# A recurrent attention and two MLPs on one core: wider token blocks in the second MLP, another transfer rate in the planner's table, earlier decay loads and a reordered range check

## The chip, the cores and the metric

The kernel runs on one NeuronCore of a Trainium2 chip. The metric is the device time of one execution in microseconds (us). The kernel uses TensorE (PE, with its weight loads shown apart as PEld), VectorE (DVE), ScalarE (ACT) and the DMA engines, whose transfers are nearly all issued from the queue of SyncE (SP). GpSimd (POOL) only fills a few constants at the start.

## The reference, cut to what matters

```python
for t in range(S):                         # per batch and head, D = 48, complex state D x D
    state = a_n[t] * state + outer(k[t], v[t])   # a_n: a scaled to a magnitude of at most 0.999
    y[t] = q[t] @ state.real
x = y as (3072 tokens, 384)
h = x @ w_in;  g = softplus(h);  x2 = g @ w_out          # first MLP, hidden width 2048
out = ((x2 @ w1) * (x2 @ w2)) @ w3 @ w_out2              # second MLP, hidden width 1024
```

There are 4 batches of 768 positions, so 3072 tokens, and 8 heads. The weights arrive as 64-bit floats.

## The kernel before, in words

**Attention.** The sequence is cut into 24 chunks of 128 positions. For chunk u, `load(u)` brings the decay inputs (a tile of 384 KB named `a`), `norm(u)` scales them, `scan` forms running complex products over pairs of chunks in a tile tagged `P`, `inv(u)` forms scaled q and k, and `mm(u)` does the matmuls (`ktp`, `sc`, `yp`, `stp`). The tile tagged `a` has one buffer; only chunk 1 borrows another (`n2`).

**First MLP.** Token blocks of 128, 256 and then seven of 384 tokens (`BLOCKS`, `NB = 384`). For each block 16 hidden slices f: `s1` multiplies into a PSUM tile `s`, ACT and DVE make the softplus, `s2a` accumulates into three PSUM tiles `acc`, and `evac` copies them out and stores them to the DRAM tiles `x2d`. The first two blocks multiply in plain float32, the others split each operand into a high and a low part in the format fp32r and use three products. Weights `wr` (32 loads of 384 KB) are turned from 64 bits to 32 by three DVE instructions.

**Second MLP.** w3 and w_out2 are first multiplied together (`w3_piece`, PSUM tile `wpa`, in three groups of columns with eight pieces k each); the split halves of w_out2 for k = 0 to 3 lie in the two buffers tagged `P`. Then come 8 blocks of 384 tokens. `b_x` loads a block of x2 and splits it (`bxh`, `bxl`, buffers `xh` and `xl` of the pool `sp`). For each of 8 slices, `s3` makes `pb` and `pa` with nine matmuls each, ACT copies `pb` to `be`, DVE multiplies (`bg`), ACT and DVE split (`bgh`, `bgl`), and `s2b` adds nine matmuls into `acc`. Five PSUM buffers of one tag serve `pa` and `pb`.

**Range check.** While the second MLP runs, all weights are loaded again (`ckr`, 80 pieces, three buffers) and DVE finds their smallest and largest squares (`ck`, `lims`). After the last matmul a few small instructions (`okp`, `ok1`, `okt`, `oki`) make one number, which every engine loads to decide whether a slow general path has to run.

**Order.** Nothing of this is issued in the order in which it is written. `Plan` records every instruction, gives it a cost and a landing time (`cost`), runs 16 rounds of list scheduling, and issues the instructions of all engines in the order of the best round. The engines then wait for semaphores only. In the table a transfer of n bytes costs at least n / 360 ns on the queue of SP, and a load of an input lands 2500 + n / 360 ns after its issue. The scheduler also knows which buffer must be free before a tile can be written.

Of the kernel before, what the change touches and what calls it, by code (L numbers as in the profile page):

```python
# [11 lines left out]
F32 = mybir.dt.float32  # L12
F32R = mybir.dt.float32r
I32 = mybir.dt.int32
AF = mybir.ActivationFunctionType
ALU = mybir.AluOpType
PSUM = bass.MemoryType.PSUM
DRAM = bass.MemoryType.DRAM

P = 128  # L20
B, H, SEQ, D = 4, 8, 768, 48
DM = H * D
NT = B * SEQ
T = 128
NCH = NT // T
CPB = SEQ // T
G = DM // P
GT = G * T
FA = 2048 // P
FB = 1024 // P  # L30
KC = DM // P
NB = 384
# [4 lines left out]
GB = 3  # L37
HB = 5
AMB = 2
ATT = 5  # L40
S1B = 5
ATAG = "s1"
YB = 1
VB = 1
# [4 lines left out]
PB = 2  # L49
XB = 2  # L50
# [4 lines left out]
LEAD = 0  # L55
ROUNDS = 16
SEED = 214
NBB = NT // NB

ROW = [128 * (_h // 2) + 64 * (_h % 2) + _d if _h < 6 else 128 * (_d // 16) + 48 + 64 * (_h - 6) + _d % 16  # L60
       for _h in range(H) for _d in range(D)]
# [10 lines left out]
class Plan:  # L72
# [49 lines left out]
    def cost(self, eng, op, outs, ins):  # L122
        n = max(self.free_size(x) for x in (*outs, *ins))
        if eng == "SP":
            size = 4
            for _, n in outs[0].ap:
                size *= n
            cost = max(650 if n < 512 and self.on_chip(ins[0]) else 475, size / 360)
            if not self.on_chip(outs[0]):
                land = 5200  # L130
            elif self.on_chip(ins[0]):
                land = 2300
            elif hasattr(ins[0].tensor, "tag_meta"):
                land = 6800
            else:
                land = 2500 + size / 360
            return cost, max(land - cost, 0)
        if eng == "PE":
            n = self.free_size(outs[0])
            if op == "transpose":  # L140
                return 109, 250
            m = outs[0].ap[0][1]
            if ins[0].dtype == F32R:
                return n / 2.4 + 14, 250
            return (0.75 * n + 24 if m <= 64 else max(n, m) / 0.6 + 5), 250
        if eng == "DVE":
            far = [x for x in ins if x.ap[-1][0] >= 4 and x.ap[-1][1] > 1]
            return 72 + n / (1.92 if op == "tensor_scalar" else 0.52 if len(far) > 1 else 0.95), 200
        if eng == "ACT":
            return 105 + 0.88 * n, 200  # L150
        return 160 + n * 2.08, 200
# [198 lines left out]
def fused(ctx: ExitStack, tc: tile.TileContext, a_in, qk_in, v_in, wio, w12, w3t, wo2, q, k, v, a_re, a_im, outT):  # L350
    nc = tc.nc
    plan = Plan(tc)
    V, A, PE, GP, SP = plan.V, plan.A, plan.PE, plan.GP, plan.SP

    fast = ExitStack()
    dram = ctx.enter_context(tc.tile_pool(name="dram", bufs=1, space=DRAM))
    x2d = [dram.tile([P, KC, NB], F32, name=f"x2d{i}", tag=f"x2d{i}") for i in range(NBB)]

    pd = [dram.tile([2 * DM, 2 * T], F32, name=f"pd{u}", tag=f"pd{u}") for u in range(NCH)]
    xg = dram.tile([DM, NT], F32, name="xg", tag="xg")  # L360
    cp = ctx.enter_context(tc.tile_pool(name="cp", bufs=1))
    wp = fast.enter_context(tc.tile_pool(name="wp", bufs=1))
    sp = fast.enter_context(tc.tile_pool(name="sp", bufs=2))
    ps = fast.enter_context(tc.tile_pool(name="ps", bufs=1, space=PSUM))
    ap = fast.enter_context(tc.tile_pool(name="ap", bufs=1))
# [3 lines left out]
    ident = cp.tile([P, P], F32, name="ident")  # L369
# [10 lines left out]
    m2max = cp.tile([P, NCH], F32, name="m2max")  # L380
    pend = cp.tile([P, B, G], F32, name="pend")
    NCK = 2 * FA + 6 * FB
    wlim = cp.tile([P, 2], F32, name="wlim")
    ncheck = [0]

# [11 lines left out]
    c = [dict() for _ in range(NCH)]  # L397
# [7 lines left out]
    def pst(tag, bufs, shape, name):  # L405
        return ps.tile(shape, F32, tag=tag, bufs=bufs, name=name)
# [3 lines left out]

    def load(u):
        s = c[u]
        s["a"] = ap.tile([P, 2, GT], F32, tag="n2" if u == 1 else "a", bufs=1, name=f"a{u}")
        SP.dma_start(s["a"], a_in[u])

    def load_qk(u):
# [268 lines left out]
    u = 0  # L685
# [6 lines left out]
    for us in groups:  # L692
        n = len(us)
# [113 lines left out]
    def s2(n, f, prods, last):  # L807
        if f == 0:
            for i in range(KC):
                acc[i] = pst(f"acc{i}", 1, [P, NB], "acc")  # L810
        for q, (w, xx) in enumerate(prods):
            for i in range(KC):
                PE.matmul(
                    acc[i][:, 0:n], w[:, i * P : (i + 1) * P], xx,
                    start=(f == 0 and q == 0), stop=(f == last and q == len(prods) - 1),
                )
# [11 lines left out]
    def s2b(f, gg):  # L828
        gh, gl = gg
        wh, wl = (x[:, (f % 2) * DM : (f % 2 + 1) * DM] for x in bwp[f // 2])  # L830
        s2(NB, f, [(wh, gh), (wl, gh), (wh, gl)], FB - 1)

    def evac(n, dst, nm):
        for i in range(KC):
            o = sp.tile([P, NB], F32, tag="e", name=f"xo{nm}_{i}")
            A.copy(o[:, 0:n], acc[i][:, 0:n])
            SP.dma_start(dst(i), o[:, 0:n])

# [82 lines left out]
    for bi in range(nblk):  # L921
        last = bi == nblk - 1
        t0, n = BLOCKS[bi]
        if not last:
            start = att_pos[0]
            goal = att_end[sum(BLOCKS[bi + 1]) // T - 1] + LEAD
        gq = {}
        for f in range(FA):
            if bi == 0:
                if f + 4 < FA:  # L930
                    w_load(f + 4)
                if f + 2 < FA:
                    w_piece(f + 2)
            gq[f] = s1(bi, f)
            if f >= 2:
                s2a(bi, f - 2, gq.pop(f - 2))
            if not last:
                att_to(start + (goal - start) * (f + 1) // FA)
            elif f >= 2:
                while pos < len(st) * (f + 1) // FA:  # L940
                    st[pos]()
                    pos += 1
                if f >= 7 and f - 7 < FB - 2:
                    w12_conv(f - 7)
        for f in (FA - 2, FA - 1):
            s2a(bi, f, gq.pop(f))
        evac(n, lambda i: x2d[t0 // NB][:, i, t0 % NB : t0 % NB + n], f"a{bi}")
    w12_conv(FB - 2)
    w12_conv(FB - 1)

    xb = {}

    def b_x(bi):
        r = ap.tile([P, 2 * H * T], F32, tag="rs1", name=f"xr{bi}")[:, 0 : KC * NB]
        r = r.rearrange("p (k n) -> p k n", k=KC)
        SP.dma_start(r, x2d[bi])
        h, l = (sp.tile([P, KC, NB], F32R, tag=t, bufs=XB, name=f"b{t}{bi}") for t in ("xh", "xl"))
        split(h, l, r)
        xb[bi] = (h, l)

    def s3(bi, f):
        xh, xl = xb[bi]
        pa = pst("s1", S1B, [P, NB], f"pa{bi}_{f}")
        pb = pst(ATAG, ATT, [P, NB], f"pb{bi}_{f}")
        wh, wl = bw[f]
        for o, c0 in ((pb, DM), (pa, 0)):
            i = 0
            for w, xx in ((wh, xh), (wl, xh), (wh, xl)):
                for k in range(KC):
                    PE.matmul(  # L970
                        o, w[:, c0 + k * P : c0 + (k + 1) * P], xx[:, k],
                        start=(i == 0), stop=(i == 3 * KC - 1),
                    )
                    i += 1
        e = sp.tile([P, NB], F32, tag="e", name=f"be_{bi}_{f}")
        A.copy(e, pb)
        g = sp.tile([P, NB], F32, tag="g", bufs=GB, name=f"bg_{bi}_{f}")
        V.tensor_tensor(out=g, in0=pa, in1=e, op=ALU.mult)
        gh = sp.tile([P, NB], F32R, tag="gh", bufs=HB, name=f"bgh_{bi}_{f}")
        gl = sp.tile([P, NB], F32R, tag="gl", bufs=HB, name=f"bgl_{bi}_{f}")  # L980
        split(gh, gl, g)
        return gh, gl

# [13 lines left out]
    for bi in range(NBB):  # L997
        gq = {}
        for f in range(FB):
            gq[f] = s3(bi, f)  # L1000
            if f >= 1:
                s2b(f - 1, gq.pop(f - 1))
            if f == 2 and bi + 1 < NBB:
                b_x(bi + 1)
            it += 1
            while ncheck[0] < min(NCK, NCK * it // nit):
                src, n = cks[ncheck[0]]
                r = raw3(src, n, f"ckr{ncheck[0]}")
                check(r, ap.tile([P, DM], F32, tag="v", bufs=VB, name=f"ck{ncheck[0]}"))
        s2b(FB - 1, gq.pop(FB - 1))  # L1010
        evac(NB, lambda i: outT[i * P : (i + 1) * P, bi * NB : (bi + 1) * NB], f"b{bi}")

    for i, n in enumerate(("min", "max")):
        V.tensor_reduce(
            out=wlim[:, i : i + 1], in_=bst[n], axis=mybir.AxisListType.X, op=getattr(ALU, n)
        )
    plan.flush()
    V, PE = nc.vector, nc.tensor
    fast.close()
    ep = ctx.enter_context(tc.tile_pool(name="ep", bufs=1))  # L1020
    okp = ep.tile([P, B * G + NCH + 2], F32, name="okp")
    c0 = 0
    for src, lim, op in (
        (pend.rearrange("p b g -> p (b g)"), 1e-3, ALU.is_ge),
# [4 lines left out]
        n = src.shape[1]  # L1029
        V.tensor_scalar(out=okp[:, c0 : c0 + n], in0=src, scalar1=lim, scalar2=None, op0=op)  # L1030
        c0 += n
    ok1 = ep.tile([P, 1], F32, name="ok1")
    V.tensor_reduce(out=ok1, in_=okp, axis=mybir.AxisListType.X, op=ALU.min)
    oki = ep.tile([1, 1], I32, name="oki")
    with tc.tile_pool(name="fps", bufs=1, space=PSUM) as fps:
        okt = fps.tile([1, P], F32, name="okt")
        PE.transpose(okt, ok1, ident)
        V.tensor_reduce(out=oki, in_=okt, axis=mybir.AxisListType.X, op=ALU.min)
    ok = nc.values_load(oki[0:1, 0:1], min_val=0, max_val=1)
    with tc.If(ok < 1):  # L1040
        general(tc, q, k, v, a_re, a_im, wio, w12, w3t, wo2, xg, outT)
# [211 lines left out]
```

## Time and profile before

| | us |
|---|---|
| median of 3 executions | 982.17 (980.64 to 984.84) |
| profiled execution, its own time | 979.78 |
| its span, first to last instruction | 978.0 |
| PE busy in the span | 883.5 (90%) |
| DVE busy in the span | 787.4 (81%) |
| granted TensorE clock, mean | 0.994 |

The profiled execution's own time is 1.8 us longer than its span. Busy time of PE is the time covered by matmuls whose ends are modelled and which overlap, so the distance from one start to the next tells what a matmul really takes.

### The profile page before, as it was taken

The numbers are of one execution on the slowest core, as the hardware profiler recorded it, in microseconds if no ns is written. First come the engines' busy times: TensorE is split into PE (matmuls) and PEld (weight loads), VectorE is DVE, ScalarE is ACT, GpSimd is POOL, SyncE is SP. The second block draws the span as 40 slices with busy tenths as digits, with TensorE's granted clock in tenths as the row PEclk, the third lists the DMA queues.
The fourth block names the chain that finished last, engine by engine and source line by source line (L and its number), as shares of the span: only waits on it lengthen the run. The fifth ranks groups of instructions, "written<-read, shape, count | busy, mean of one in ns | idle before, by whom it ended". The sixth has DMA issues, their size and how long they took to land.

```text
span 978.0 us, 16869 instructions
## 1 busy us (share of the span) xinstructions
PE 883.5 (90%) x6169; PEld 859.3 (88%) x6169; DVE 787.4 (81%) x1773; ACT 529.5 (54%) x1132; POOL 5.4 (1%) x13
## 2 busy tenths in 40 slices
PE   0027999899999999999999999999999999999996
PEld 0027888799999999999999999999999999999996
DVE  7999999999999999999888787899788975312212
ACT  4246776677877795876766666833222223323221
POOL 2000000000000000000000000000000000000000
PEclk9998999999999999999999999999999999999999
DMA  9763736444573644537262855375788783000000
GB/s 343 244 170 66 189 96 139 125 107 112 164 161 95 161 108 133 156 72 200 82 166 73 191 165 153 106 200 186 250 251 265 238 252 123 24 26 25 1 25 28
DMA packets 84619, 138.68 MB, mean 142 GB/s; under 512 B 8112, under 2 KB 56880, under 8 KB 84528
## 3 DMA queue, kind: packets, MB, share of 16 engines
q1 hardware_dynamic: 84528, 137.53, 50.1%
q8 instruction: 50, 0.82, 0.4%
q14 instruction: 41, 0.34, 0.1%
HBM read 108.00 MB, written 28.31 MB: 139 GB/s over the span
## 4 chain that ended last, share of the span: by engine, by line
PE 64%; DVE 10%; DMA 7%; issue 2%; ACT 1%; SPq 0%; DVEq 0%; ACTq 0%
PE acc L194 23%; PE s L194 14%; PE pa L194 8%; PE pb L194 8%; PE sc L194 3%; PE yp L194 3%; PE wpa L194 3%; DMA a<-a_in 2%; DVE tm L194 2%; DMA ckr<-wio 2%; DVE P L194 2%; DMA ckr<-w 1%; PE stp L194 1%; DVE ck L194 1%; DVE g L194 1%
## 5 line engine op out<-in xcount | busy, mean ns | idle before, releaser
L194 DVE TENSOR_TENSOR tm<-P 128x90 f32<-128x90 f32 (+3 forms) x240 | 145.8, 616 | 1.1
L194 ACT ACTIVATE e<-e 128x384 f32<-128x384 f32 (+2 forms) x288 | 136.2, 486 | 2.9
L194 DVE TENSOR_TENSOR bg<-pa,be 128x384 f32<-128x384 f32 x64 | 35.3, 555 | 91.2 <-PE pa L194 68.4
L194 ACT ACTIVATE e<-s 128x384 f32<-128x384 f32 (+2 forms) x144 | 64.3, 450 | 44.4 <-PE s L194 37.2
L194 DVE TENSOR_TENSOR P<-tm 128x45 f32<-128x45 f32 (+11 forms) x304 | 85.8, 343 | 1.3
L194 ACT CAST bgh<-bg 128x384 fp32r<-128x384 f32 x64 | 32.7, 514 | 93.1 <-DVE bg L194 93.0
L194 DVE SCALAR_TENSOR_TENSOR g<-s,e 128x384 f32<-128x384 f32 (+2 forms) x144 | 73.3, 513 | 12.0 <-ACT e L194 11.8
L194 PE MATMUL ktp<-ident,qkp 128*128 128x128 f32 x120 | 20.9, 289 | 66.0 <-DVE qkp L194 64.4
L194 PEld LDWEIGHTS ktp<-ident,qkp 128*128 128x128 f32 x120 | 15.6, 148 | 68.6 <-issue 57.5
L194 ACT CAST gh<-g 128x384 fp32r<-128x384 f32 x112 | 56.5, 509 | 25.1 <-DVE g L194 18.3
L194 ACT COPY be<-pb 128x384 f32<-128x384 f32 x64 | 30.5, 480 | 71.6 <-PE pb L194 68.7
L194 DVE TENSOR_TENSOR gl<-g,gh 128x384 fp32r<-128x384 f32 x112 | 61.8, 559 | 4.4 <-ACT gh L194 2.7
L194 DVE CUSTOM_DVE_ANT_0 ck<-ckr 128x384 f32<-128x384 f32 x80 | 43.4, 543 | 19.2 <-DMA ckr<-wio 6.5
L194 PE MATMUL sc<-rs 112*128 112x128 f32 x384 | 53.0, 285 | 4.3 <-ACT y L194 1.7
L194 PEld LDWEIGHTS sc<-rs 112*128 112x128 f32 x384 | 50.3, 198 | 6.2 <-ACT y L194 1.9
L194 DVE TENSOR_TENSOR bgl<-bg,bgh 128x384 fp32r<-128x384 f32 x64 | 35.2, 555 | 15.8 <-ACT bgh L194 15.6
L194 DVE TENSOR_REDUCE lims<-ck 128x1 f32<-128x384 f32 x80 | 43.0, 537 | 2.0
L194 PE MATMUL yp<-am,v 128*48 128x128 f32 x384 | 36.9, 282 | 4.4 <-issue 3.2
L194 ACT COPY xob<-acc 128x384 f32<-128x384 f32 x24 | 11.4, 481 | 52.5 <-PE acc L194 37.4
L194 PE MATMUL wpa<-wo,w 128*128 128x384 f32 x192 | 39.1, 334 | 0.0
L194 PE MATMUL s<-x,w 128*128 128x128 f32 (+1 forms) x192 | 36.0, 330 | 3.1 <-ACT x L194 2.2
L194 ACT ACTIVATE nt<-a 128x768 f32<-128x768 f32 x24 | 20.3, 845 | 31.9 <-DMA a<-a_in 31.8
(323 smaller groups left out, 2581.3 us busy)
## 6 DMA issues: line engine op xcount, KB each, us to landing
pd<-qkp SPq DMA_DIRECT2D x24, 768.0 KB, 4.4
rs<-pd SPq DMA_DIRECT2D x48, 384.0 KB, 6.1
wr<-wio SPq DMA_DIRECT2D x32, 384.0 KB, 5.5
ckr<-wio SPq DMA_DIRECT2D x32, 384.0 KB, 3.6
a<-a_in SPq DMA_DIRECT2D x24, 384.0 KB, 3.7
qk<-qk_in SPq DMA_DIRECT2D x24, 384.0 KB, 3.9
w3r<-w3t SPq DMA_DIRECT2D x16, 384.0 KB, 3.5
w12r<-w SPq DMA_DIRECT2D x16, 384.0 KB, 3.3
```

The source lines that it names most:

```text
L194: getattr(engine.unit, op)(*args, **kw)
```

## The change

- The second MLP works in 6 blocks of 512 tokens. Each block is read from one or two of the `x2d` tiles. Its split halves lie in the two `P` buffers (even blocks) or in `wb6` and `wb7` (odd blocks). `be` and `bg` share one tile out of `wa12` to `wa15`, which also hold the evacuated outputs, and `bgh` and `bgl` share one buffer of `xh` or `xl`, four in turn.
- The planner's table counts transfers at 270 bytes per ns in place of 360, in the queue's cost and in the landing time of inputs.
- The decay inputs of chunks 2 and 3 have buffers of their own (`xl`), so their loads need not wait for an earlier chunk.
- The last instructions of the range check are recorded in the plan, and use buffers that are already there, instead of being issued after it in new ones.

```diff
+NX = 512
+NBB = NT // NX
...
-            cost = max(650 if n < 512 and self.on_chip(ins[0]) else 475, size / 360)
+            cost = max(650 if n < 512 and self.on_chip(ins[0]) else 475, size / 270)
...
-                land = 2500 + size / 360
+                land = 2500 + size / 270
...
     def load(u):
         s = c[u]
-        s["a"] = ap.tile([P, 2, GT], F32, tag="n2" if u == 1 else "a", bufs=1, name=f"a{u}")
+        if u in (2, 3):
+            t = sp.tile([P, KC, NB], F32, tag="xl", bufs=XB, name=f"a{u}")
+            s["a"] = t.rearrange("p k n -> p (k n)")[:, 0 : 2 * GT].rearrange("p (c n) -> p c n", c=2)
+        else:
+            s["a"] = ap.tile([P, 2, GT], F32, tag="n2" if u == 1 else "a", bufs=1, name=f"a{u}")
...
     def b_x(bi):
...
-        SP.dma_start(r, x2d[bi])
-        h, l = (sp.tile([P, KC, NB], F32R, tag=t, bufs=XB, name=f"b{t}{bi}") for t in ("xh", "xl"))
+        n0 = 0
+        while n0 < NX:
+            i, o = divmod(bi * NX + n0, NB)
+            n = min(NB - o, NX - n0)
+            SP.dma_start(r[:, :, n0 : n0 + n], x2d[i][:, :, o : o + n])
+            n0 += n
+        if bi % 2:
+            h, l = (wp.tile([P, KC, NX], F32R, tag=f"wb{i}", name=f"bx{i}_{bi}") for i in (6, 7))
+        else:
+            h, l = (ap.tile([P, KC, NX], F32R, tag="P", bufs=PB, name=f"bx{i}_{bi}") for i in "hl")
...
+    def b_room(name):
+        return wp.tile([P, 2 * DM], F32, tag=f"wa{12 + next(nbf) % 4}", name=name)[:, 0:NX]
+
+    def b_pair(name):
+        t = sp.tile([P, KC, NB], F32R, tag=("xh", "xl")[next(nbg) % 2], bufs=XB, name=name)
+        t = t.rearrange("p k n -> p (k n)")
+        return t[:, 0:NX], t[:, NX : 2 * NX]
...
-        e = sp.tile([P, NB], F32, tag="e", name=f"be_{bi}_{f}")
-        A.copy(e, pb)
-        g = sp.tile([P, NB], F32, tag="g", bufs=GB, name=f"bg_{bi}_{f}")
-        V.tensor_tensor(out=g, in0=pa, in1=e, op=ALU.mult)
-        gh = sp.tile([P, NB], F32R, tag="gh", bufs=HB, name=f"bgh_{bi}_{f}")
-        gl = sp.tile([P, NB], F32R, tag="gl", bufs=HB, name=f"bgl_{bi}_{f}")
+        g = b_room(f"bg_{bi}_{f}")
+        A.copy(g, pb)
+        V.tensor_tensor(out=g, in0=pa, in1=g, op=ALU.mult)
+        gh, gl = b_pair(f"bgg_{bi}_{f}")
         split(gh, gl, g)
...
-    plan.flush()
-    V, PE = nc.vector, nc.tensor
-    fast.close()
-    ep = ctx.enter_context(tc.tile_pool(name="ep", bufs=1))
-    okp = ep.tile([P, B * G + NCH + 2], F32, name="okp")
+    okp = ap.tile([P, DM], F32, tag="v", bufs=VB, name="okp")
...
+    okt = pst("s1", S1B, [P, NB], "okt")[0:1, 0:P]
+    PE.transpose(okt, ok1, ident)
+    V.tensor_reduce(out=oki, in_=okt, axis=mybir.AxisListType.X, op=ALU.min)
+    plan.flush()
+    fast.close()
```

## Rows read from the trace of the kernel before

**Rows 1.** Part 1 of the page: busy time, share, instructions.

```profile
PE 883.5 (90%) x6169; PEld 859.3 (88%) x6169; DVE 787.4 (81%) x1773; ACT 529.5 (54%) x1132; POOL 5.4 (1%) x13
```

**Rows 2.** Windows by stage: from:to length, busy of each engine, PEclk, DMA share, GB/s.

```profile
0.00:57.50 57.50, 0.00 (x0) 0.01 (x1) 51.06 (x106) 18.39 (x32) 5.42 (x13) 1.00 0.75 265
57.50:125.00 67.50, 51.09 (x520) 47.66 (x520) 65.94 (x152) 43.63 (x108) 0.00 (x0) 0.95 0.59 142
...
200.00:655.00 455.00, 450.92 (x3438) 441.36 (x3437) 416.34 (x911) 326.77 (x697) 0.00 (x0) 1.00 0.52 135
655.00:700.00 45.00, 45.00 (x261) 45.00 (x260) 42.31 (x105) 15.80 (x32) 0.00 (x0) 1.00 0.68 211
700.00:800.00 100.00, 96.12 (x545) 94.02 (x545) 81.83 (x216) 25.27 (x51) 0.00 (x0) 1.00 0.83 254
800.00:961.00 161.00, 161.00 (x930) 160.85 (x929) 53.74 (x111) 43.20 (x86) 0.00 (x0) 1.00 0.14 45
```

**Rows 3.** Waits of PE, whole span: total us, times, longest.

```profile
PE ktp L194 <- DVE qkp L194: 64.4, 2, 57.5
PE s L194 <- ACT xh L194: 4.4, 3, 1.9
...
PE pb L194 <- DVE bg L194: 2.0, 2, 1.5
PE pa L194 <- DVE bg L194: 1.8, 1, 1.8
```

**Rows 4.** The chain that ended last, its end: start us, us, what.

```profile
961.54 8.34 PE acc L194 x48
...
969.90 0.38 DVE okp L1030 x4
...
970.96 0.28 DVE oki L1038
```

**Rows 5.** Timeline of PE in the float32 block of 256 tokens.

```profile
141.76 1.89 PE L194 MATMUL s<-x,w 128*128 128x256 f32 x8
143.49 1.46 PE L194 MATMUL acc<-g,w 128*128 128x256 f32 x6
```

**Rows 6.** Groups by form: a sixth of the acc matmuls of the second MLP.

```profile
L194 PE MATMUL acc<-bgh,bwp2h 128*128 128x384 f32 x96 | 31.5, 335 | 0.0
```

**Rows 7.** Waits of DVE from 655 to 800 us.

```profile
DVE ck L194 <- DMA ckr<-wio: 6.5, 8, 2.2
DVE ck L194 <- DMA ckr<-w: 4.6, 5, 2.6
DVE ck L194 <- DMA ckr<-w3t: 3.7, 5, 1.9
```

**Rows 8.** Tile ckr: the check's first pass, min/median/max ns, first and last start.

```profile
L194 DVE CUSTOM_DVE_ANT_0 ck<-ckr x80: 416/558/561, 680.9 to 818.4; 128x384 f32<-128x384 f32 x72, 128x256 f32<-128x256 f32 x8
```

**Rows 9.** Part 6 of the page: loads, KB each, median us to landing.

```profile
wr<-wio SPq DMA_DIRECT2D x32, 384.0 KB, 5.5
...
a<-a_in SPq DMA_DIRECT2D x24, 384.0 KB, 3.7
```

**Rows 10.** Waits of ACT and of DVE in the first 200 us.

```profile
ACT nt L194 <- DMA a<-a_in: 23.4, 7, 6.0
...
DVE nt L194 <- ACT nt L194: 7.2, 4, 4.8
```

**Rows 11.** The chain's longest wait for a decay load.

```profile
446.98 7.02 DMA a<-a_in
```

**Rows 12.** Tiles pb, then pa, from 655 to 671 us; tile w3t there.

```profile
655.00:671.00 16.00, 5.58 (x27) 4.58 (x26) 1.45 (x3) 1.00 0.61 192
...
655.00:671.00 16.00, 6.11 (x26) 4.65 (x26) 1.11 (x2) 1.00 0.61 192
...
L194 DVE TENSOR_TENSOR w<-w3t,w x8: 415/420/422, 655.8 to 672.2; 128x256 fp32r<-128x256 f32 x8
```

**Rows 13.** Timeline of SP at the end: the last output transfers.

```profile
965.26 5.52 SPq L194 DMA_DIRECT2D outT<-xob  x3
```

More of the change, by code (lines that the diff above doesn't have):

```diff
@@ L57 @@
 SEED = 214
-NBB = NT // NB
+NBA = NT // NB
+NX = 512
+NBB = NT // NX
 ROW = [128 * (_h // 2) + 64 * (_h % 2) + _d if _h < 6 else 128 * (_d // 16) + 48 + 64 * (_h - 6) + _d % 16
@@ L356, in fused @@
     dram = ctx.enter_context(tc.tile_pool(name="dram", bufs=1, space=DRAM))
-    x2d = [dram.tile([P, KC, NB], F32, name=f"x2d{i}", tag=f"x2d{i}") for i in range(NBB)]
+    x2d = [dram.tile([P, KC, NB], F32, name=f"x2d{i}", tag=f"x2d{i}") for i in range(NBA)]
     pd = [dram.tile([2 * DM, 2 * T], F32, name=f"pd{u}", tag=f"pd{u}") for u in range(NCH)]
@@ L382, in fused @@
     NCK = 2 * FA + 6 * FB
+    oki = cp.tile([1, 1], I32, name="oki")
     wlim = cp.tile([P, 2], F32, name="wlim")
@@ L809, in s2 @@
             for i in range(KC):
-                acc[i] = pst(f"acc{i}", 1, [P, NB], "acc")
+                acc[i] = pst(f"acc{i}", 1, [P, NX], "acc")
         for q, (w, xx) in enumerate(prods):
@@ L830, in s2b, with evac @@
         wh, wl = (x[:, (f % 2) * DM : (f % 2 + 1) * DM] for x in bwp[f // 2])
-        s2(NB, f, [(wh, gh), (wl, gh), (wh, gl)], FB - 1)
-    def evac(n, dst, nm):
+        s2(NX, f, [(wh, gh), (wl, gh), (wh, gl)], FB - 1)
+    def evac(n, dst, nm, room):
         for i in range(KC):
-            o = sp.tile([P, NB], F32, tag="e", name=f"xo{nm}_{i}")
+            o = room(f"xo{nm}_{i}")
             A.copy(o[:, 0:n], acc[i][:, 0:n])
@@ L946, in fused @@
             s2a(bi, f, gq.pop(f))
-        evac(n, lambda i: x2d[t0 // NB][:, i, t0 % NB : t0 % NB + n], f"a{bi}")
+        evac(n, lambda i: x2d[t0 // NB][:, i, t0 % NB : t0 % NB + n], f"a{bi}",
+             lambda name: sp.tile([P, NB], F32, tag="e", name=name))
     w12_conv(FB - 2)
@@ L953, in b_x @@
     def b_x(bi):
-        r = ap.tile([P, 2 * H * T], F32, tag="rs1", name=f"xr{bi}")[:, 0 : KC * NB]
+        r = ap.tile([P, 2 * H * T], F32, tag="rs1", name=f"xr{bi}")[:, 0 : KC * NX]
         r = r.rearrange("p (k n) -> p k n", k=KC)
-        SP.dma_start(r, x2d[bi])
-        h, l = (sp.tile([P, KC, NB], F32R, tag=t, bufs=XB, name=f"b{t}{bi}") for t in ("xh", "xl"))
+        n0 = 0
[8 more added lines that the diff above has]
+            h, l = (ap.tile([P, KC, NX], F32R, tag="P", bufs=PB, name=f"bx{i}_{bi}") for i in "hl")
         split(h, l, r)
         xb[bi] = (h, l)
+    nbf, nbg = count(), count()
+    def b_room(name):
[4 more added lines that the diff above has]
+        return t[:, 0:NX], t[:, NX : 2 * NX]
     def s3(bi, f):
         xh, xl = xb[bi]
-        pa = pst("s1", S1B, [P, NB], f"pa{bi}_{f}")
-        pb = pst(ATAG, ATT, [P, NB], f"pb{bi}_{f}")
+        pa = pst("s1", S1B, [P, NX], f"pa{bi}_{f}")
+        pb = pst(ATAG, ATT, [P, NX], f"pb{bi}_{f}")
         wh, wl = bw[f]
@@ L1010, in fused @@
         s2b(FB - 1, gq.pop(FB - 1))
-        evac(NB, lambda i: outT[i * P : (i + 1) * P, bi * NB : (bi + 1) * NB], f"b{bi}")
+        evac(NX, lambda i: outT[i * P : (i + 1) * P, bi * NX : (bi + 1) * NX], f"b{bi}", b_room)
     for i, n in enumerate(("min", "max")):
@@ L1031, in fused @@
         c0 += n
[L1032 to L1038, printed above, removed]
+    ok1 = okp[:, DM - 1 : DM]
+    V.tensor_reduce(out=ok1, in_=okp[:, 0:c0], axis=mybir.AxisListType.X, op=ALU.min)
+    okt = pst("s1", S1B, [P, NB], "okt")[0:1, 0:P]
[3 more added lines that the diff above has]
+    fast.close()
     ok = nc.values_load(oki[0:1, 0:1], min_val=0, max_val=1)
```

## The prediction

> **What bounds the kernel now.** I read the page first, then the windows by stage, then who PE waits for, then the chain's end. PE is busy 90% of the span [rows 1], and the windows say where it is not: it does nothing for the first 57.5 us, while DVE is busy 51.06 of them; it is covered by three quarters from 57.5 to 125 us; and from 200 us on the only stretch with a visible hole is 700 to 800 us, 96.12 of 100 [rows 2]. From 655 us on, the second MLP, PE is the bound, with 3.8 us of waits for `bg` [rows 3]. So a saving in the time of its matmuls there counts in full. From 200 to 655 us PE and DVE are both close to full (450.92 and 416.34 of 455) [rows 2], and the order in which DVE does its work is as important as the amount. Before 125 us the first product waits behind DVE: 57.5 us before the first transposes [rows 3].
>
> **The width of 512.** In the second MLP a slice has 9 + 9 + 9 = 27 matmuls, so 8 blocks x 8 slices x 27 = 1728 before (576 of them `acc`, of which [rows 6] is a sixth), and 6 x 8 x 27 = 1296 after, with the same number of columns in all. The duration of 335 ns in the group is no measure, since matmuls overlap; the last 48 of them, with nothing between, take 8.34 us [rows 4], 173.75 ns each. At the granted clock of 1.00, the level of 2.4 GHz, 384 columns at one a cycle are 160 ns, so 13.75 ns are over. What 512 columns take, no row shows. If the rest is a fixed cost for each matmul, it is 213.3 + 13.75 = 227.1 ns; if it grows with the columns, 173.75 x 512 / 384 = 231.7 ns; and if it belongs to this width alone, the nearest row from the other side is the float32 block, whose instructions of 256 columns follow each other in (143.49 - 141.76) / 8 = 216 ns [rows 5], close to 512 cycles. Before: 1728 x 0.17375 = 300.2 us. After: 294.3, 300.2 or 279.9 us. So the gain is 5.9 us, between 0 and 20.3. I take 5.9: every matmul brings a weight load of the same size whatever its width, which speaks for a fixed part.
>
> The Trainium skill (TensorE: Matmul & The Clock Gate, Back-to-back issue gap) gives a gap of N / 2.4 + 2.5 ns for warm matmuls. That is 162.5 ns for 384 columns, which this trace contradicts with its 173.75, and 215.8 ns for 512; by it alone the gain would be 1728 x 162.5 less 1296 x 215.8 ns, 1.1 us, as an estimate from that page.
>
> ACT and DVE get fewer, wider instructions there, and DVE is busy only 53.74 of 161 us from 800 us on [rows 2], so their cost is nothing on the path; if that cover went, six blocks would still do the same elements. The four buffers for `be`, `bg` and outputs, and four instead of five for the split pairs, are behind the same cover. PE's reserve grows: five PSUM buffers of which two are in use leave three, 27 matmuls of PE time, 6.1 us instead of 4.7 us.
>
> **The table's 270 bytes per ns, second MLP.** The check's 80 pieces start over 680.9 to 818.4 us [rows 8], 1.72 us apart. The plan before allowed 393,216 / 360 = 1.09 us for a load, the new one allows 1.46 us, so about six tenths of the error go away. DVE stands in its fixed order and waited 6.5 + 4.6 + 3.7 = 14.8 us for these loads [rows 7]; behind it stands `bg`, and behind `bg` PE, 3.8 us [rows 3]. I take 2 us off; the bounds are 0 and 3.8.
>
> **The same table, the rest.** In the first stages the loads of chunk inputs land a median 3.7 us after issue [rows 9], up to 7.0 us [rows 11]; the plan's 3.6 us becomes 4.0 us. All orders change with it. What can be gained from 200 to 655 us is PE's open time, 455 - 450.92 = 4.1 us [rows 2]; a loss of the same size is as well possible. I take 1 us off, since the new figure is nearer to what landed.
>
> **Early decay loads.** Chunks 2 and 3 can load at the start. ACT waited 23.4 us for such loads in the first 200 us, but ACT is not the bound; DVE behind it waited 7.2 us, of which 4.8 us is the first wait, for chunk 0 [rows 10], and that load does not change. So 2.4 us at most. Against it: SP's queue is shared, two loads of 393,216 bytes at the 265 bytes per ns of that stretch [rows 2] are 3.0 us that weights may come later. I take 1 us off, bounds 2.4 off and 3.0 on.
>
> **The start of the second MLP.** Before, `b_x(0)` used free buffers and `pb` began at about 655 us, while the last group of `w3_piece` was still going (its splits run from 655.8 to 672.2 us) [rows 12]. Now its halves must wait for the two `P` buffers, and these hold the split w_out2 of k = 0 to 3, which that last group reads. From 655 to 671 us PE had 27 + 26 = 53 matmuls of `pb` and `pa` [rows 12], 9.2 us of work that it can't have then if the order stays. The planner knows the buffers' owners and can bring the w3 pieces forward; two thirds of the products need only the high half, free after k = 1. I charge 1.5 us, bounds 0 and 9.2. The wait stands in ACT's and DVE's queues at the split, with softplus work of the first MLP's last block behind it.
>
> **The tail.** The range check's last work ran from 969.90 to 971.24 us, after the last matmul at 969.88 [rows 4]. Moved into the plan, it is done before. But SP issues its last output until 965.26 + 5.52 = 970.78 us [rows 13] and must then load the same number, so only 0.5 us were the check's, and the last copy is a third wider. I take 0.3 us off; bounds 0 and 1.4.
>
> **Sum.** 979.8 - 5.9 - 2 - 1 - 1 + 1.5 - 0.3 = 971.1 us for the profiled execution. The median of the runs shown is 2.4 us above that one, so the forecast is 973.5 us as a median, 0.9% less. About 0.5%, 4.9 us, is what a measurement of this kernel can tell from no change; the three executions differ by 4.2 us.
>
> **The rivals**, as medians:
> - *The start of the second MLP stalls in full.* PE idles the 9.2 us. For it: DVE is busy 42.31 of 45 us there [rows 2], so there is little room to hurry. Against it: the scheduler's freedom before. 973.5 + 7.7 = 981.2 us, no change.
> - *Matmuls grow with their columns.* The gain of 5.9 us is gone: 979.4 us, no change. For it: no row has two widths of fp32r. Against it: the weight load. In this case the wide blocks do not do what they are for.
> - *512 columns take the 216 ns of the float32 row.* 973.5 - 14.4 = 959.1 us. For it: 216 ns is near 512 cycles. Against it: 384 columns are not near 384 cycles, so a weight load of fp32r seems to cost more than one of float32. The Trainium skill's rule above (same page and section) would give this distance.
> - *Slower: the plan's first stage becomes bound by loads.* At the new rate the plan counts 0.364 us more for each 384 KB load. The 32 loads `wr` [rows 9] and the eight of the first four chunks are 40 x 0.364 = 14.6 us more in the plan, and DVE's fixed order would put work that these loads feed that much later, though the chip moved 265 bytes per ns as a mean over the first 57.5 us with the DMA engines 75% busy [rows 2], so they could go faster. Then the first full matmuls come later by the same amount. Without the terms of the first stages the sum is 979.8 - 5.9 - 2 + 1.5 - 0.3 + 14.6 = 987.7, as a median 990.1 us. It makes the kernel slower once the delay is over 11.6 us. Against it: DVE is the bound there and has other work to fill in.
>
> **How the numbers follow.** The forecast has a chance of 0.50, the full stall 0.17, growth with columns 0.12, 216 ns 0.08, the slow first stage 0.13. Within the forecast the open terms spread it from 966 to 981 us, so a tenth and more of it is no change. Faster by over 0.5%: 0.43 of the forecast, the 0.08, and 0.07 where a rival meets a good order, 0.58. Slower by over 0.5%: the 0.13 and a little of the stall, 0.15. The rest, 0.27, is no change. The range leaves out the 216 ns and half of the slow first stage: 964 to 987 us.
>
> **What would show it.** Right: `acc`, `pa` and `pb` as 128x512 with starts 227 ns apart; PE waits for `bg` under 2 us and fewer DVE waits for `ckr`, whose pieces start further apart; no `okp` after the last matmul, and a span that ends some 7.8 us after the last matmul instead of 8.1; the first `pb` beside `wpa` without a hole. Wrong: starts 216 or 231 ns apart; a hole of PE between the last `acc` of the first MLP and the first `pb`; a first transpose later than 57.5 us, or less PE time covered from 57.5 to 125 us than 51.09 us. What I can least see is the new order as a whole: if stage times between 57.5 and 655 us move by more than 5 us, the prediction fails there and not in the second MLP.

## The result and the profile after

The changed kernel takes 971.03 us (970.29 to 971.47) beside 982.71 us for the kernel before, a ratio of 0.9884 with a 95% interval of 0.9861 to 0.9907. Measured again on another chip, beside other runs, it was 0.9896 (0.9872 to 0.9921). The forecast was 973.5 us, the range 964 to 987. The profiled execution took 971.33 us with a span of 969.6 us, 8.4 us less than the span before. The medians differ by more, 11.7 us, because the profiled execution of the kernel before was 2.9 us faster than its median; the account below is of the two profiled executions.

First the page of the changed kernel, part 1, and its windows by stage, as in [rows 1, 2].

```profile
PE 879.0 (91%) x5737; PEld 810.7 (84%) x5737; DVE 786.4 (81%) x1739; ACT 525.5 (54%) x1092; POOL 5.4 (1%) x13
...
0.00:57.50 57.50, 0.00 (x0) 0.00 (x0) 50.74 (x106) 18.46 (x31) 5.43 (x13) 1.00 0.73 263
57.50:125.00 67.50, 48.52 (x460) 46.23 (x460) 64.82 (x145) 44.33 (x108) 0.00 (x0) 0.95 0.61 147
125.00:200.00 75.00, 70.61 (x458) 63.78 (x459) 73.72 (x172) 51.49 (x118) 0.00 (x0) 0.93 0.50 129
200.00:655.00 455.00, 452.46 (x3449) 444.30 (x3448) 420.47 (x926) 328.22 (x702) 0.00 (x0) 1.00 0.53 135
...
655.00:700.00 45.00, 45.00 (x217) 39.38 (x216) 40.01 (x91) 15.75 (x27) 0.00 (x0) 1.00 0.73 217
...
700.00:800.00 100.00, 100.00 (x443) 82.84 (x442) 80.92 (x198) 25.89 (x41) 0.00 (x0) 1.00 0.79 241
...
800.00:955.00 155.00, 155.00 (x685) 128.38 (x685) 53.38 (x103) 38.01 (x62) 0.00 (x0) 1.00 0.16 51
```

The hole from 700 to 800 us is closed, 100.00 of 100 in place of 96.12, with DVE as busy as before. The first stages did not gain: PE is covered for 48.52 us between 57.5 and 125 us where it was 51.09, and from 125 to 200 us its granted clock is 0.93 where it was 1.00. In the second MLP PEld falls well below PE, 82.84 of 100: fewer matmuls mean fewer loads of weights for the same columns.

The chain's end, the waits of PE over the whole span, the wide matmuls by group, and the first wide products:

```profile
956.39 5.91 PE acc L196 x26
962.30 0.02 issue
962.33 0.59 ACT xob L196
```

```profile
PE ktp L196 <- DVE qkp L196: 66.2, 3, 58.6
PE s L196 <- ACT x L196: 4.4, 1, 4.4
PE sc L196 <- DMA rs<-pd: 4.2, 2, 3.1
```

```profile
L196 PE MATMUL acc<-bgg,bwp0h 128*128 128x512 f32 x144 | 49.9, 389 | 0.0
```

```profile
L196 PE MATMUL pb<-bxh,bw0h x18: 389/389/398, 660.9 to 869.0; 128*128 128x512 f32 x18
```

The last 26 matmuls take 5.91 us, 227.3 ns each, while the group says 389 ns: again the distance counts and not the duration. No row of PE's waits names `bg` any more, against 3.8 us in [rows 3]. The longest wait, 58.6 us for the first transposes, is 1.1 us longer than before. The first `pb` comes at 660.9 us, some 6 us later than before [rows 12], and PE is full around it.

DVE's waits for the check's loads from 655 to 800 us, and the check's first pass, beside [rows 7, 8]:

```profile
DVE ck L196 <- DMA ckr<-wio: 4.9, 6, 1.5
...
DVE ck L196 <- DMA ckr<-w3t: 3.8, 5, 1.7
DVE ck L196 <- DMA ckr<-w: 1.8, 2, 1.2
```

```profile
L196 DVE CUSTOM_DVE_ANT_0 ck<-ckr x80: 416/558/564, 679.9 to 828.7; 128x384 f32<-128x384 f32 x72, 128x256 f32<-128x256 f32 x8
```

They wait 10.5 us in place of 14.8 (15.5 with 0.7 us for `wo`, which [rows 7] leaves out), and the 80 pieces start 1.86 us apart in place of 1.72.

The end of the span, by the timeline of all engines:

```profile
961.86 1.41 SPq L196 DMA_DIRECT2D outT<-xob  x2
961.90 0.39 PE L196 MATMUL acc<-bgg,bwp2h 128*128 128x512 f32 x1
962.13 0.27 PE L196 MATMUL okt<-ident,okp 128*1 128x128 f32 x1
962.33 0.59 ACT L196 COPY xob<-acc 128x512 f32<-128x512 f32 x1 [0.49 <-PE acc L196]
962.43 0.28 DVE L196 TENSOR_REDUCE oki<-okt 1x1 int32<-1x128 f32 x1 [3.86 <-PE okt L196]
```

The small `okp` instructions run at 830 us now, but the transpose `okt`, for which only `oki` waits, has the last place on PE in the plan. So `oki` is still made after the last matmul, at 962.71 us, before SP has issued its last output at 963.27 us. From the last matmul to the end it is 969.6 - 962.30 = 7.3 us, where it was 978.0 - 969.88 = 8.1.

Where the 8.4 us of the span came from: the second MLP's matmuls 1728 x 173.75 - 1296 x 227.3 ns, 5.7 us less; PE's waits in it 3.8 us less; the tail 0.8 us less; and what is left over by subtraction, 1.9 us more, put down to the stages before 655 us. Of these 1.9 us the windows show 0.7 us. PE's covered time from 57.5 to 655 us is 48.52 + 70.61 + 452.46 us, where it was 51.09 + 70.25 + 450.92, and the first matmul, 1.1 us later, is part of that. The rest does not show as uncovered time. Covered time counts a matmul at the lower clock in full, so the clock of 0.93 from 125 to 200 us may be where it lies; this is not shown. The window before was:

```profile
125.00:200.00 75.00, 70.25 (x432) 61.81 (x432) 74.09 (x171) 54.52 (x126) 0.00 (x0) 1.00 0.51 132
```

### The profile page after: what moved, and what is told of

Read it like the earlier page. It is cut to its first block, busy times and chain, and to the rows that moved or that the text cites. A ratio compares the mean times of both kernels' runs of the same rounds, so it can differ in the third digit from the quotient of the medians.

```text
span 969.6 us, 15873 instructions
## 1 busy us (share of the span) xinstructions
PE 879.0 (91%) x5737; PEld 810.7 (84%) x5737; DVE 786.4 (81%) x1739; ACT 525.5 (54%) x1092; POOL 5.4 (1%) x13
## 4 chain that ended last, share of the span: by engine, by line
PE 85%; DVE 11%; DMA 1%; issue 1%; ACT 1%; SPq 0%; DVEq 0%; ACTq 0%
PE acc L196 30%; PE s L196 22%; PE pb L196 10%; PE pa L196 10%; PE yp L196 3%; PE wpa L196 3%; PE sc L196 3%; DVE P L196 3%; DVE tm L196 3%; DVE w L196 2%; PE stp L196 2%; PE ktp L196 1%; DVE am L196 1%; DMA wr<-wio 1%; DVE qkp L196 1%
## 5 line engine op out<-in xcount | busy, mean ns | idle before, releaser
L196 DVE TENSOR_TENSOR bg<-pa,bg 128x512 f32<-128x512 f32 x48 | 33.1, 690 | 89.7 <-PE pa L196 69.5
L196 DVE SCALAR_TENSOR_TENSOR g<-s,e 128x384 f32<-128x384 f32 (+2 forms) x144 | 73.3, 512 | 10.2 <-ACT e L196 8.1
L196 ACT CAST bgg<-bg 128x512 fp32r<-128x512 f32 x48 | 29.8, 621 | 95.4 <-DVE bg L196 95.4
L196 ACT COPY bg<-pb 128x512 f32<-128x512 f32 x48 | 28.2, 587 | 90.6 <-PE pb L196 90.5
L196 PE MATMUL acc<-bgg,bwp0h 128*128 128x512 f32 x144 | 49.9, 389 | 0.0
L196 PE MATMUL acc<-bgg,bwp2h 128*128 128x512 f32 x144 | 47.7, 389 | 0.0
L196 DVE TENSOR_TENSOR bgg<-bg,bgg 128x512 fp32r<-128x512 f32 x48 | 33.0, 688 | 15.6 <-ACT bgg L196 15.5
L196 PE MATMUL s<-x,w 128*128 128x128 f32 (+1 forms) x192 | 39.0, 351 | 4.4 <-ACT x L196 4.4
```

The source lines that it names most:

```text
L196: getattr(engine.unit, op)(*args, **kw)
```

## The experiments

Theory: the gain is the fixed part of each matmul (5.9 us) and the waits behind the check's loads, which the table's rate takes away. Rivals: the width's larger reserve in PSUM removes those waits by itself; the small parts (early loads, range check) have a gain or a cost of their own; the new order as a whole is what counted. All ratios are to the kernel before on the same chip, where it took medians of 980.19 to 982.71 us.

| kernel | median us | ratio (95% interval) | PE waits after 655 us | DVE waits for `ckr` |
|---|---|---|---|---|
| before | 982.71 | 1 | 3.8 | 17.2 |
| changed, again | 970.67 | 0.9896 (0.9872 to 0.9921) | 0 | 12.9 |
| rate 270 alone | 975.36 | 0.9950 (0.9932 to 0.9969) | 0.9 | 18.0 |
| early loads alone | 985.79 | 1.0051 (1.0034 to 1.0067) | 5.1 | 19.4 |
| range check alone | 994.90 | 1.0144 (1.0117 to 1.0171) | 2.5 | 18.7 |
| changed, rate 360 | 977.44 | 0.9972 (0.9959 to 0.9986) | 2.2 | 16.3 |
| changed, no early loads | 970.08 | 0.9899 (0.9877 to 0.9920) | 0 | 11.8 |
| changed, old range check | 973.73 | 0.9939 (0.9917 to 0.9960) | 0 | 10.5 |
| changed, blocks of 384 | 978.62 | 0.9986 (0.9972 to 1.0000) | 0 | 11.2 |
| before, seed 1 | 986.47 | 1.0059 (1.0039 to 1.0078) | 4.0 | 19.3 |
| before, seed 2 | 985.06 | 1.0044 (1.0026 to 1.0062) | 2.3 | 18.8 |
| changed, seed 1 | 971.03 | 0.9901 (0.9875 to 0.9926) | 0 | 10.0 |
| changed, rate 230 | 970.82 | 0.9884 (0.9865 to 0.9903) | 0 | 5.4 |

The last two columns are sums over the rows of the waits, in us: PE's on the second MLP's products from 655 to 966 us, without the transpose of the range check, and DVE's for `ckr` from 650 to 840 us. The width alone, with the old table and the old check, gave no time. So its part is read from the distances of the starts, and from the changed kernel with blocks of 384.

**Rate 270 alone.** In the kernel before:

```diff
-            cost = max(650 if n < 512 and self.on_chip(ins[0]) else 475, size / 360)
+            cost = max(650 if n < 512 and self.on_chip(ins[0]) else 475, size / 270)
...
-                land = 2500 + size / 360
+                land = 2500 + size / 270
```

> The kernel before with the table at 270 bytes per ns alone. My theory: PE's waits for bg in the second MLP fall from 3.8 to about 1.5 us, and the stages before move by 2 us or less either way: ratio 0.996 to 1.000. Rival (PE's waits went by the width alone): waits for bg stay near 3.8 us, ratio 1.000 or the new order of the first stages shows, 1.000 to 1.004. Rival (the first stage becomes bound by loads): first matmul several us after 57.5 us, ratio over 1.005.

0.9950, somewhat better than expected. PE's waits after 655 us and DVE's for `ckr` from 655 to 830 us:

```profile
PE pb L194 <- DVE bg L194: 0.9, 1, 0.9
```

```profile
DVE ck L194 <- DMA ckr<-w3t: 7.9, 5, 4.6
DVE ck L194 <- DMA ckr<-wio: 6.6, 5, 3.5
DVE ck L194 <- DMA ckr<-wo: 3.3, 4, 1.9
```

PE's waits go from 3.8 to 0.9 us with blocks of 384, so the rate does it here without the width. But DVE waits for the loads as long as before. What has changed is not how long DVE stands, but whether PE needs what stands behind it.

**Early loads alone.** In the kernel before:

```diff
     def load(u):
         s = c[u]
-        s["a"] = ap.tile([P, 2, GT], F32, tag="n2" if u == 1 else "a", bufs=1, name=f"a{u}")
+        if u in (2, 3):
+            t = sp.tile([P, KC, NB], F32, tag="xl", bufs=XB, name=f"a{u}")
...
```

> The kernel before with only the two buffers for the decay inputs of chunks 2 and 3. My theory: within 2.4 us less and 3 us more, ratio 0.998 to 1.003, since DVE is the bound there and gets the same work. Rival (the first stage waits for these loads): first matmul earlier by 2 us or more, ratio 0.997 or less.

1.0051, above the forecast's bounds, with the first matmul at 58.9 us. Whether that is the loads' doing, the run without them below tells.

**Range check alone.** The last instructions of the check in the plan of the kernel before, as in the change.

> The kernel before with only the last range check instructions in the plan. My theory: the time from the last matmul of the MLP to the end of the span falls from 8.1 us to about 7.5 us and nothing else moves: ratio 0.999 to 1.0. Rival (order noise): more than 2 us either way although the work is the same.

1.0144. The tail did what was expected, 988.1 - 980.5 = 7.6 us in place of 8.1. But the kernel is 13.9 us slower by the medians, and its profiled execution, the fastest of the five, is 10.1 us slower. The loss lies elsewhere; the windows of this kernel from 57.5 us on:

```profile
57.50:125.00 67.50, 46.76 (x422) 43.80 (x423) 64.23 (x144) 44.80 (x103) 0.00 (x0) 0.85 0.62 142
125.00:200.00 75.00, 69.70 (x488) 61.31 (x487) 72.51 (x164) 47.27 (x113) 0.00 (x0) 1.00 0.47 116
200.00:655.00 455.00, 447.59 (x3410) 437.78 (x3409) 415.62 (x917) 328.20 (x700) 0.00 (x0) 1.00 0.52 135
```

From 57.5 to 655 us PE is covered 8.2 us less than before (46.76 + 69.70 + 447.59 beside 51.09 + 70.25 + 450.92), and from 57.5 to 125 us its granted clock was 0.85 where it was 0.95: it stood at half speed, 1.2 GHz, for a longer part of a stretch in which PE had been idle before and then worked with gaps. In windows of 5 us the clock was 0.50 from 80 to 90 us, with PE covered 3.35 and 1.05 us, while the kernel before had 0.72 and 0.93 there with 3.27 and 4.31 us. A check that runs after 800 us changed the first 200 us, because the planner's order is one whole. The planner draws one random number for each instruction in its noisy round; a likely way, not shown, is that a few more instructions shift all draws.

**Changed, rate 360.**

```diff
-            cost = max(650 if n < 512 and self.on_chip(ins[0]) else 475, size / 270)
+            cost = max(650 if n < 512 and self.on_chip(ins[0]) else 475, size / 360)
...
-                land = 2500 + size / 270
+                land = 2500 + size / 360
```

> The changed kernel with the table back at 360. Theory (the table removes DVE's waits for the check's loads, as it did alone, 3.8 to 0.9 us of PE waits from 655 us on): with blocks of 512 some wait of PE for bg comes back, 1 to 3 us; in all 2 to 6 us slower than the changed kernel, ratio to before 0.990 to 0.995. Rival (the wide blocks' reserve hides DVE's waits by itself): no PE wait after 655 us, ratio 0.987 to 0.990.

0.9972, some 7 us slower than the changed kernel and more than the 2 to 6 us expected. PE's waits from 655 to 960 us:

```profile
PE acc L196 <- ACT bgg L196: 2.2, 3, 1.3
```

So the wide blocks' reserve does not remove PE's waits by itself: 2.2 us are back, now for the split `bgg` that ACT makes. The rest of the spans' difference, 975.3 - 969.6 - 2.2 = 3.5 us, lies elsewhere, in the first stages for the most part, since the matmuls and the tail are the same and PE is covered 3.1 us less from 57.5 to 655 us.

**Changed, no early loads.**

```diff
-        if u in (2, 3):
-            t = sp.tile([P, KC, NB], F32, tag="xl", bufs=XB, name=f"a{u}")
...
+        s["a"] = ap.tile([P, 2, GT], F32, tag="n2" if u == 1 else "a", bufs=1, name=f"a{u}")
```

> The changed kernel without the buffers for the decay inputs of chunks 2 and 3. If the parts add up as they stood alone (this one alone was 1.0051): ratio to before 0.983 to 0.985. Rival (what a small part did alone was the luck of the order it led to): the difference to the changed kernel, 0.9884, has another size or sign, within 1% either way.

0.9899, no different from the changed kernel's 0.9896. The kernel before with the loads alone was 0.5% slower, but taken out of the changed kernel they give nothing: the parts don't add up.

**Changed, old range check.** The last instructions after the plan and in a pool of their own, as before.

> The changed kernel with the old range check after the plan. If the parts add up as they stood alone (this one alone was 1.0144): ratio to before about 0.974, 957 us. Rival (luck of the order): not that; by the work alone the tail is 0.8 us longer again, 8.1 in place of 7.3 us, ratio 0.987 to 0.991 with the order's spread around it.

0.9939. Here the part is worth 3.1 us by the medians (4 us by the ratios), ten times what was forecast, and the chain's end shows why:

```profile
960.29 0.59 ACT xob L196
960.88 0.02 issue
960.90 2.00 DMA outT<-xob
962.90 0.04 DVEq L1053
...
963.09 0.38 DVE okp L1053 x4
...
964.10 0.28 DVE oki L1061
```

`okp` waits until the last output has landed, 2.00 us. In the kernel before it waited for the last matmul only [rows 4]. The new pool of the check gets memory that the closed pools gave back, and with the change the outputs lie in `wa12` to `wa15`, so by the wait the new tile overlaps one of them. That overlap is inferred from the wait and not read from addresses. The tail is 970.5 - 960.27 = 10.2 us, 2.9 us longer than in the changed kernel.

**Changed, blocks of 384.**

```diff
-NX = 512
+NX = 384
```

> The changed kernel with blocks of 384 tokens in the second MLP, all else as changed (new buffers, 270, early loads, new check). Theory (width gives 5.8 us by the fixed part of each matmul): second MLP's starts 173 ns apart, 5.8 us slower than the changed kernel plus a PE wait or two for bg, ratio to before 0.994 to 0.998. Rival (the gain came from elsewhere): within 2 us of the changed kernel.

0.9986, 8 us slower than the changed kernel and just above the 0.994 to 0.998 expected. Its last matmuls by the chain:

```profile
964.31 4.87 PE acc L196 x28
```

That is 173.9 ns each, with no wait of PE after 655 us. By these distances 5.7 to 6.0 us of the difference are the matmuls; the last one ends at 969.18 us, 6.9 us later than in the changed kernel.

**Seeds.** One number in the planner, in the kernel before twice (1, then 2) and in the changed kernel once (1):

```diff
-SEED = 214
+SEED = 1
```

> The kernel before with another seed for the one round of noise in the planner, so the same instructions in another order. Theory (the order alone moves the time by as much as the small parts did alone): ratio away from 1 by 0.3 to 1.5%, with the difference in PE's lost time before 655 us and none in the matmuls' distances. Rival (the order hardly counts, and the early loads and the range check had a cost of their own): within 0.2% of 1.

> As the run before it, with a third seed: by the order theory another value in the range 0.995 to 1.015; by the rival within 0.2% of 1.

> The changed kernel with the other seed. If the width (5.8 us) and the table's share in the second MLP (3 to 4 us) are properties of the change and not of one lucky order: no PE wait after 655 us again, starts 227 ns apart, and 5 to 13 us less than the kernel before with this same seed. If the gain was the order's luck: no difference to the kernel before with this seed.

The same instructions in another order: 1.0059 and 1.0044, with the loss in the first stages and the waits of the second MLP still there. These are the window from 57.5 to 125 us and the wait of PE of the kernel before with seed 1:

```profile
57.50:125.00 67.50, 46.49 (x449) 43.35 (x450) 65.41 (x152) 44.73 (x106) 0.00 (x0) 0.92 0.59 146
```

```profile
PE pb L194 <- DVE bg L194: 3.8, 3, 2.5
```

The changed kernel with that seed is at 0.9901, with no wait after 655 us. With one seed the change is worth 15.4 us, more than the 5 to 13 us expected; with the other it is worth about 10 to 12.

**The changed kernel, beside them.**

> The changed kernel itself, beside the following three on one chip. Expected: ratio to before 0.987 to 0.991, as measured first.

0.9896, as measured first.

**Changed, rate 230.** `size / 270` becomes `size / 230` at both places.

> The changed kernel with the table at 230 bytes per ns, which is what the check's loads really got in it (393,216 bytes each 1.8 to 1.9 us would be 210 to 220). Theory (the table helped by removing DVE's waits, and with 270 PE has no wait left after 655 us): nothing more to gain there, DVE's waits for ckr fall further without effect, ratio to before 0.985 to 0.995 by the order's spread. Rival (a truer table also orders the first stages better): PE's lost time before 655 us falls by 3 us or more, ratio 0.986 or less.

970.82 us, ratio 0.9884: DVE's waits for `ckr` fall to 5.4 us and nothing is gained, since PE did not wait for them any more. The check's pieces start from 680.0 to 841.3 us, 2.02 us apart.

## Why the prediction was right

The forecast of 973.5 us and its sum of 8.7 us for the profiled execution stand beside 971.03 and 8.4. The 2.5 us by which the median lies lower are the 2.4 us that were added because the median before lay above its profiled execution; in the changed kernel the two agree within 0.3 us. The likeliest case came, but the sum is so close by luck: three terms came out 3.8 us better than taken, the others 4.1 us worse, and these nearly cancel. The terms are these.

- *The width, 5.9 us.* Right: 5.7 us, starts of 227.3 ns where 227.1 was worked out with a fixed part. Both other prices are out, 231.7 and 216 ns. That the fixed part is the weight load is not shown, since no run changes the load alone. The planner of the kernel before already prices an fp32r matmul of n columns at n / 2.4 + 14 ns (in `cost`), which the prediction did not use. The Trainium skill (TensorE: Matmul & The Clock Gate, Back-to-back issue gap) gives 215.8 ns for 512 columns by the rule quoted in the prediction, 11.5 ns less than this trace's 227.3. The same section gives that rule for a single matmul by itself and names about 131 ns at 512 columns for a stream of weight loads and matmuls, which this trace contradicts too.
- *The table in the second MLP, 2 us.* The step was under-sized, 3.8 us, and its mechanism half right. All six kernels with a rate of 360 have 2.2 to 5.1 us of PE waits after 655 us, all seven with 270 or 230 have 0 to 0.9. But I reasoned that DVE would wait less; with the rate alone it waits as long (18.0 beside 17.2 us), and yet PE does not wait. Which place in DVE's order spares PE was not looked into further.
- *The table in the rest and the early loads, 1 us each.* Neither came: the first stages lost 1.9 us. (The 7.0 us that the prediction gives for a decay load of the first stages is a wait at 447 us [rows 11].) The experiments do not give either part a proven cost or gain of its own in the first stages; two other seeds move the kernel before by 4 to 6 us with no change in its work, as much as the early loads did alone. But the kernel before seems to have a lucky order: of the six kernels at 360 its PE has the most covered time from 57.5 to 655 us, 572.3 us, the others 564.1 to 569.8. Those at 270 or 230 have 569.0 to 574.3. So the new rate may gain some 3 us there that this seed hides; the two groups overlap, and it is not shown.
- *The start of the second MLP, 1.5 us on.* Nothing: PE had 45.00 of 45 us there, though the first `pb` came 6 us later: from 655 to 661 us it did 17 products of `wpa` and 19 of the first MLP's `acc`, where the kernel before did 12 and 7. The full stall is out.
- *The tail, 0.3 us.* 0.8 us. A likely reason, not shown, is that all engines but SP may go on earlier. Against the change without this part it is worth about 3 us, by a wait for the last output that I had not seen: with the new place of the outputs the old check waits longer.
- *The slow first stage.* The first matmul is 1.1 us later, not 11.6 or more, and the rate alone made the kernel faster.

What I said I could see least, the order as a whole, moved by 1.9 us and stayed below the 5 us I named. That was partly luck: the range check alone moved it by more than 8. Two of the signs that I named for being wrong did come, the first transposes after 57.5 us (58.6) and less than 51.09 us covered from 57.5 to 125 us (48.52); in the first stages the prediction was wrong, and the second MLP and the tail carried the gain.

## What to carry to other kernels

Where TensorE is the bound and each matmul carries a fixed cost, work out the fixed part from the distance of starts and widen the moving operand as far as the buffers allow; here the gain was read ahead to within half a microsecond. Where a planner writes the order, a part's effect measured alone is the part plus a new order: compare it with what another seed does before giving it a cost, and test it by leaving it out of the whole as well. The seed of the kernel before may itself be a lucky one. A transfer rate in such a planner is good enough once nobody behind the loads waits. The distance at which the loads come does not tell the true rate by itself, because it follows the table: the check's pieces, each behind a load of 393,216 bytes, started 1.72 us apart at 360, 1.86 at 270 and 2.02 at 230.

## What was not expected of the hardware

A matmul of fp32r took 13.75 ns over its columns at 384 and 227.3 - 213.3 = 14.0 ns at 512, while the float32 instructions of 256 columns followed each other 216 ns apart [rows 5], within 3 ns of 512 cycles. And an order with other gaps on PE early can be paid for in clock as well: with the range check alone PE was covered 46.76 us from 57.5 to 125 us with a granted clock of 0.85, against 51.09 us and 0.95. The sum of the gaps does not decide it: the changed kernel with blocks of 384 was covered still less there, 45.61 us, at a clock of 0.97. What decides it was not looked into.
